# Half of an expert's first weight loaded earlier, and unread matmuls and a new order in the first units of a fused recurrence and mixture-of-experts kernel

## The chip, the cores and the metric

The kernel runs on one core of one Trainium2 chip. The metric is device time in microseconds (us) of one execution, taken as the median of several. PE is the matrix engine (PEld its weight loads), DVE the vector engine, ACT the scalar engine, POOL the GpSimd engine, SP the sync engine, which issues the loads of the two large inputs and the stores. POOL issues the loads of the expert weights, and these convert float32 to bfloat16 on the way.

## The reference

Two stages follow each other. The first is a gated recurrence over 5056 steps, for 4 sequences of 256 channels; the second is a soft mixture of experts with 8 experts of 4 slots each, over all 20224 tokens.

```python
sig = 1 / (1 + exp(-f_logit));  f = lb + (1 - lb) * sig
for t in range(S):  h = f[:, t] * h + (1 - f[:, t]) * x[:, t];  y[:, t] = h
logits = y @ phi                               # 20224 x 32
d = softmax(logits, over tokens);  slot_input = d.T @ y
slot_out[e] = relu(slot_input[e] @ w1[e]) @ w2[e]     # w1: 256x1024, w2: 1024x256
out = softmax(logits, over slots) @ slot_out
```

The inputs `x` and `f_logit` are 20.7 MB each, the weights 16.8 MB, the output 20.7 MB, all float32.

## The kernel before

The program has a stage that reads and a stage that writes. The sequences are cut into 10 groups of 512 steps; a group of one sequence is a unit, so that there are 40 units (`n_unit`). The loop `for n in range(n_unit)` writes the order of every engine by hand (`manual_schedule`), so that an instruction stands on its engine where the loop puts it.

What happens to a unit, in the order of its data:

- `load` (L207): SP loads `f_t` and `x_t`, six units ahead, into three buffers each. The first four units have loads of their own (`SINGLE` = 4), later ones go in pairs.
- `gate` (L226): ACT takes the sigmoid of `f_t` into `s_t`.
- `enter` (L236): POOL multiplies `s_t` by `x_t` into `u_t` (DVE does it for unit 0).
- `s_to_channels`, `u_to_channels` (L266, L275): PE turns both so that channels lie on partitions, into `sp` and `up` in PSUM. From unit 4 on a unit's `up` needs the `u_t` of both units of its pair (`half_to_channels`, L260).
- `decay` (L288): ACT makes the factors `a` from `sp`.
- `scan` (L323): DVE runs the recurrence, two scans of 512 steps for each unit (L332).
- `to_tokens`, `keep_tokens` (L339, L355): PE turns the result `h` back, and DVE or ACT copies it to `ht`.
- Then `logits`, `exps`, `weights_to_tokens` and `slots` add each group to `slot_ps`, one half of a PSUM bank.

The other half of that bank, `slot_bank[:, 1]`, takes matmuls that nobody reads: `idle(k)` (L177) puts k of them, `ident_f` by `wide_rep` with 256 columns in float32, into PE's order. `wide_rep` is a view of `rep`, which POOL builds in four copies (`rep_constants`, L84).

POOL issues the weight loads in its own order of work, after `enter(n + 3)` of the units that a table names. Entries 0 to 7 are `w1` of each expert, 8 to 15 are `w2`; the last `w2` goes in three pieces:

```python
W_AT = {9: 1, 17: 1, 25: 1, 31: 1, 32: 1, 33: 2, 34: 3, 36: 6}
```

After the last unit come the slot inputs (`sin_ps`, a part of the PSUM tile `tail`, in which PE also writes the row sums), the hidden layer (`hi`, from `w1`), its turned copies (`hid`, `wide`), the sums over `w2` (L684, and L696 into `so_ps`), `slot_out` (L708), and then the stage that writes: PE multiplies the stored weights of each token by `slot_out`, DVE and ACT scale the product by the row sums, SP stores it.

Of the kernel before, what the change touches and what calls it, by code (L numbers as in the profile page):

```python
# [18 lines left out]
def kernel(  # L19
# [10 lines left out]
    nc = tc.nc  # L30
# [5 lines left out]
    P = 128  # L36
# [47 lines left out]
    def rep_constants(b):  # L84
        blk = ident_f[ds(b * NS, NS), ds(b * NS, NS)]
        nc.gpsimd.tensor_copy(rep[ds(b * NS, NS)], blk.unsqueeze(1).broadcast_to([NS, B, NS]))
# [17 lines left out]
    def lb_constants():  # L104
        row = lb_row.rearrange("u (p o) -> u p o", o=DC)
        lb_ps = ptp.tile([P, R, P], F32, name="lb_ps", tag="tp")
        lb = lb_ps[:, 0, ds(0, DC)]
        for o in range(DC):
            nc.tensor.transpose(lb_ps[:, 0, ds(o, 1)], row[:, :, o], ident_f[ds(0, 1), ds(0, 1)])
        nc.vector.tensor_scalar(omlb, lb, -1.0, 1.0, ALU.mult, ALU.add)  # L110
        nc.vector.tensor_scalar(nomlb, lb, 1.0, -1.0, ALU.mult, ALU.add)
# [22 lines left out]

    def load_w(i):
        if i < E:
            nc.gpsimd.dma_start(out=w1_sb[i], in_=w1_r[i])
        else:
            if i == 2 * E - 2:
                t = ld.tile([P, 2, R, D], F32, name="w_t", tag="f_t")  # L140
                t = t.rearrange("p u r d -> p (u r d)").bitcast(BF16).rearrange(
                    "p (e f d) -> p e f d", e=2, f=FC)
                w2_sb.extend(t[:, i] for i in range(2))
            parts = (FC // 2, FC // 4, FC // 4) if i == 2 * E - 1 else (FC,)
            for j, k in enumerate(parts):
                f = sum(parts[:j])
                nc.gpsimd.dma_start(out=w2_sb[i - E][:, ds(f, k)], in_=w2_r[i - E][:, ds(f, k)])
# [14 lines left out]
    with tc.tile_pool(name="sp2", bufs=3) as sp2, \  # L162
# [11 lines left out]

        wide_rep = rep.rearrange("p b s -> p (b s)").unsqueeze(1).broadcast_to([P, 2, P])

        def idle(k, first=False):  # L177
            if first:
                for i in range(2):
                    nc.tensor.matmul(slot_bank[:, 1, ds(0, P)], ident, ident,  # L180
                                     start=True, stop=False, skip_group_check=True)
            for _ in range(k):
                nc.tensor.matmul(slot_bank[:, 1], ident_f, wide_rep,  # L183
                                 start=False, stop=False, skip_group_check=True)
        xs, fs, sts, uts, pss, psus, hs, hps, hts, lgs, ets = ({} for _ in range(11))

# [70 lines left out]
                nc.tensor.matmul(v[:, :, :, r], t(r)[k].bitcast(F32), sides,  # L257
                                 is_transpose=True, start=True, stop=True)

        def half_to_channels(n, ps, t):  # L260
            k = ds(n % 2 * (P // 2), P // 2)
            v = ps.rearrange("c p r -> c (p r)").rearrange("c (p r) -> c p r", r=2 * R)
            for r in range(2 * R):
                nc.tensor.transpose(v[:, :, r], t(r)[k].bitcast(F32), ident_f[k, k])  # L264

        def s_to_channels(n):  # L266
# [8 lines left out]
        def u_to_channels(n):  # L275
            ps = psu.tile([P, P, R], F32, name="up", tag="up")
            if long(n):
                half_to_channels(n, ps, lambda r: uts[n - n % 2 + r // R][:, r % R])
            elif n // B == odd:
                woven_to_channels(n, ps, lambda r: uts[n - n % 2 + r // R][:, r % R])  # L280
            else:
                to_channels(n, ps, uts[n])
            psus[n] = ps.rearrange("c p r -> c (p r)").bitcast(BF16).rearrange(
                "c (t o) -> c t o", o=DC)
# [149 lines left out]
        def unit(f, m):  # L434
            if 0 <= m < n_unit:
                f(m)
# [45 lines left out]
            load(n, 1)  # L482
        load(SINGLE)
        lb_constants()
        gate(0, 1)
        enter(0)
        s_to_channels(0)
        decay(0, 1, [0])
        u_to_channels(0)
        gate(1, 1)  # L490
        decay(0, 1, [1])
        phi_constants()
        enter(1)
        s_to_channels(1)
        u_to_channels(1)
        gate(2, 1)
        decay(1, 1)
        enter(2)
        for n in range(n_unit):
            if n < SINGLE - 2:  # L500
                if n:
                    unit(to_tokens, n - 1)
                    unit(u_to_channels, n + 1)
                s_to_channels(n + 2)
                if n + 3 < SINGLE:
                    gate(n + 3, 1)
                decay(n + 2, 1)
                if n + 3 == SINGLE:
                    gate(n + 3)
                if n % 2 == 0:  # L510
                    unit(load, n + AHEAD)
                unit(enter, n + 3)
                for b in range(2 * n, 2 * n + 2):
                    rep_constants(b)
            else:
                end = n >= n_unit - 6
                if n % 2 == 0:
                    unit(load, n + AHEAD)
                    if n == SINGLE - 2:
                        to_tokens(n - 1)  # L520
                        keep_tokens(n - 1)
                    if not end and n >= SETTLED:
                        unit(gate, n + 4)
                else:
                    unit(decay, n + 1)
                    if n in (late + 1, late + 3):
                        keep_tokens(n - 2)
                    if n < SETTLED:
                        gate(n + 3)
                    if n == n_unit - 5:  # L530
                        gate(n + 3)
                        exps(odd - 1)
                if not end and n != n_unit - 7:
                    group(exps, n - 2)

                unit(enter, n + 3)
                for _ in range(W_AT.get(n, 0)):
                    load_w(w_next[0])
                    w_next[0] += 1

                if n in (n_unit - 3, n_unit - 2):
                    unit(u_to_channels, n + 1)
                if n in (late, late + 2):
                    to_tokens(n - 2)
                elif n not in (SINGLE - 2, late - 1, late + 1):
                    unit(to_tokens, n - 1)
                if n == n_unit - 2:
                    keep_tokens(n - 1)
                if n % 2 == 0:
                    unit(s_to_channels, n + 2)  # L550
                    unit(s_to_channels, n + 3)
                if n not in (n_unit - 3, n_unit - 2):
                    unit(u_to_channels, n + 1)
                if n in (n_unit - 5, n_unit - 4):
                    idle(2)
                elif n == SINGLE - 2:
                    idle(1, True)
                elif 2 * B <= n < n_unit - 4 and n % (2 * B) in (1, 5, 6, 7):
                    idle(1)
                if n == n_unit - 2:  # L560
                    tail = psp.tile([P, 2, G], F32, name="tail", tag="sp")
                    sums = tail[:, 0]
                    rs_ps = sums[:, ds(0, n_grp * R * B)].rearrange(
                        "p (q b) -> p q b", b=B)
                    late_ps, odd_ps = (
                        tail[:, 1].bitcast(BF16)[:, ds(i * R * P, R * P)].rearrange(
                            "p (r s) -> p r s", r=R) for i in range(2))
                    logits(odd)
                    exps(odd)
                    slots(odd - 2)  # L570
                elif not end and by_pairs(n - 1):
                    if n % B == 0:
                        g = (n - 1) // (2 * B) * 2
                        for i in range(2):
                            logits(g + i, [2, 3] if n % (2 * B) == 0 else [0, 1])
                elif not end:
                    group(logits, n - 1)
            if n == n_unit - 1:
                odd_weights()
                logits(last, [0, 1, 2])  # L580

            unit(scan, n)
            if n in (late, late + 2):
                keep_tokens(n - 2)
                to_tokens(n - 1)
            elif n not in (SINGLE - 2, late - 1, late + 1, n_unit - 2):
                unit(keep_tokens, n - 1)
            if n == n_unit - 3:
                weights_to_tokens(odd - 1, nc.scalar.copy)
            elif not n >= n_unit - 6:  # L590
                group(weights_to_tokens, n - 3)
                batch(slots, n - 4, 0)
                batch(slots, n - 4, 1)
                if n > 2 * B and n % (2 * B) == 3:
                    idle(1)
# [17 lines left out]
        slot_sb = hpool.tile([P, G, DC], BF16, name="slot_sb", tag="h")  # L613
        slot_sb = slot_sb.rearrange("p t o -> p (t o)").bitcast(F32)[:, ds(0, D)]
        nc.vector.tensor_copy(slot_sb, slot_ps)
        sin_ps = tail[:, 0, ds(G // 2, DC * NS)].rearrange("p (o s) -> p o s", o=DC)
        slot_v = slot_sb.rearrange("p (c o) -> p o c", o=DC)
        for o in range(DC):
            nc.tensor.matmul(sin_ps[:, o], slot_v[:, o], rep[:, 0],
# [250 lines left out]
```

## Time and profile before

| what | value |
|---|---|
| median of 3 runs | 197.94 us (197.11, 197.94, 198.4) |
| the profiled execution, its own time | 197.01 us |
| its span, from the first to the last instruction | 195.2 us |
| busy share of the span: PE, DVE, ACT, POOL | 77%, 73%, 71%, 53% |
| read from HBM, written to it | 58.23 MB, 20.71 MB |
| mean granted clock of PE, as a share of full speed | 0.845 |

The span is 1.8 us shorter than the execution's own time. The shares are averages over two stages: up to about 142 us the kernel reads and computes, after it it writes. So the table says little by itself, and stages must be read one by one. In the views, a line "A <- B: 3.5, 2, 2.6" of waits says that A waited for B 3.5 us in total, 2 times, at most 2.6 us. In the table of stretches, each engine has its busy time and, as (x..), its number of instructions; behind them stand PE's granted clock, the mean busy share of the 16 DMA engines and GB/s moved. Those bytes are counted as they are written, so that a weight, read in float32 and written in bfloat16, counts half.

### The profile page before, as it was taken

The page shows a single profiled execution, that of the slowest core. Times are in us where ns is not written, and L with a number is a line of the kernel's source. Part 1 is how long each engine was busy: PE and PEld are TensorE (multiplying, and loading weights), DVE is VectorE, ACT ScalarE, POOL GpSimd, SP SyncE. Part 2 cuts the span into 40 slices and gives each one's busy share as a digit, 9 for nine tenths or more (in the row PEclk, how much of TensorE's full clock was granted, in tenths as well). Part 3 has the DMA queues.
Part 4 walks back from the last instruction along what each step waited for, and adds up shares of the span by engine and source line. Part 5 has one row for each costly group of instructions (what it writes and reads, how often), then busy time and mean ns, then how long its engine had stood idle before and what let it go on. Part 6 is the DMA issues. An engine that isn't in the chain of part 4 may idle for free.

```text
span 195.2 us, 3283 instructions
## 1 busy us (share of the span) xinstructions
PE 150.6 (77%) x1222; PEld 108.7 (56%) x1222; DVE 142.0 (73%) x175; ACT 138.8 (71%) x192; POOL 103.1 (53%) x78
## 2 busy tenths in 40 slices
PE   0684896898998979989798976999997999980000
PEld 0474775765786657857576755766872663420000
DVE  2666699799699999999999999824288867770000
ACT  3686778599988998989988698724068788991000
POOL 2584888756798949776888979592030000000000
PEclk9998799699699999999999999999985555555555
DMA  6999999999999999999999999999949999999995
GB/s 203 415 433 428 426 425 421 430 426 411 326 428 426 423 334 405 423 425 414 324 418 418 235 212 214 214 212 211 170 165 428 425 431 426 430 433 430 430 430 218
DMA packets 12145, 70.75 MB, mean 362 GB/s; under 512 B 1361, under 2 KB 1874, under 8 KB 7650
## 3 DMA queue, kind: packets, MB, share of 16 engines
q1 hardware_dynamic: 9504, 62.13, 76.3%
q0 software_dynamic: 2624, 8.42, 21.8%
q8 instruction: 9, 0.15, 0.3%
q14 instruction: 6, 0.05, 0.1%
q10 hardware_dynamic: 2, 0.00, 0.0%
HBM read 58.23 MB, written 20.71 MB: 404 GB/s over the span
## 4 chain that ended last, share of the span: by engine, by line
PE 36%; DVE 28%; DMA 17%; ACT 4%; issue 4%; SPq 1%; POOL 0%; ACTq 0%
DVE h L332 17%; DMA w_t<-in_moe_w_dram 7%; PE op L801 7%; PE sp L249 7%; PE op L727 6%; DMA w_sb<-in_moe_w_dram 6%; PE hp L345 5%; DVE ht L364 5%; PE up L264 4%; DMA f_t<-in_f_logit_dram 4%; DVE h L319 3%; DVE oc L717 2%; PE op L760 2%; ACT s_t L234 1%; PE lg L378 1%
## 5 line engine op out<-in xcount | busy, mean ns | idle before, releaser
L245 POOL TENSOR_TENSOR u_t<-s_t,x_t 128x1024 bf16<-128x1024 bf16 (+1 forms) x39 | 82.4, 2129 | 24.5 <-ACT s_t L234 14.2
L332 DVE TENSOR_TENSOR_SCAN h<-a,h,up 128x512 bf16<-128x512 f32 x64 | 78.1, 1267 | 9.0 <-PE up L264 4.3
L234 ACT ACTIVATE s_t<-f_t 128x2048 bf16<-128x2048 f32 (+2 forms) x22 | 38.1, 1736 | 2.9 <-DMA f_t<-in_f_logit_dram 2.9
L345 PE MATMUL hp<-ident_f,h 128*128 128x128 f32 (+1 forms) x160 | 29.3, 307 | 8.4 <-DVE ht L364 6.3
L297 ACT ACTIVATE a<-sp,lbs 128x1024 f32<-128x1024 bf16 x28 | 29.6, 1112 | 4.6 <-PE sp L249 4.5
L345 PEld LDWEIGHTS hp<-ident_f,h 128*128 128x128 f32 (+1 forms) x160 | 23.2, 206 | 17.0 <-DVE ht L364 11.5
L249 PE MATMUL sp<-ident_f,s_t 128*128 128x128 f32 x144 | 23.7, 315 | 7.0 <-ACT s_t L234 5.7
L249 PEld LDWEIGHTS sp<-ident_f,s_t 128*128 128x128 f32 x144 | 19.6, 164 | 8.7 <-ACT s_t L234 6.5
L264 PE MATMUL up<-ident_f,u_t 64*128 64x64 f32 x224 | 21.4, 236 | 2.4 <-POOL u_t L245 2.4
L264 PEld LDWEIGHTS up<-ident_f,u_t 64*128 64x128 f32 x224 | 17.0, 144 | 7.1 <-POOL u_t L245 2.8
L721 ACT ACTIVATE ob<-op,rrow 128x256 f32<-128x256 f32 x32 | 12.4, 478 | 9.1 <-PE op L727 8.7
L364 ACT COPY ht<-hp 128x512 f32<-128x512 f32 (+1 forms) x21 | 12.2, 583 | 7.9 <-PE hp L345 7.9
L304 ACT ACTIVATE a<-sp,lbs 128x512 f32<-128x512 bf16 (+2 forms) x16 | 13.2, 868 | 2.9 <-PE sp L249 2.7
L183 PE MATMUL slot_ps<-rep,ident_f 128*128 128x256 f32 x42 | 14.2, 426 | 0.0
L364 DVE COPY ht<-hp 128x512 f32<-128x512 f32 (+1 forms) x19 | 12.7, 668 | 1.0 <-PE hp L345 1.0
L801 PE MATMUL op<-slot_bd,etall 64*128 64x512 bf16 x32 | 13.1, 627 | 0.0
L812 ACT ACTIVATE oc<-op,rrow 128x256 f32<-128x256 f32 x32 | 12.2, 486 | 0.8 <-PE op L801 0.3
L727 PE MATMUL op<-slot_out,etall 32*128 32x256 bf16 x64 | 12.6, 375 | 0.1
L806 DVE TENSOR_TENSOR oc<-op,rrow 128x1024 f32<-128x1024 f32 x8 | 9.7, 1223 | 3.4 <-PE op L801 3.4
L717 DVE TENSOR_TENSOR ob<-op,rrow 128x1024 f32<-128x1024 f32 (+2 forms) x12 | 9.8, 862 | 2.2 <-DMA out_dram<-ob 1.1
L727 PEld LDWEIGHTS <-etall 32*128 32x128 bf16 x64 | 8.9, 153 | 3.8 <-issue 1.3
L378 PE MATMUL lg<-h,phi 128*32 128x512 bf16 (+1 forms) x80 | 9.9, 389 | 0.2 <-ACT et L402 0.2
(109 smaller groups left out, 168.9 us busy)
## 6 DMA issues: line engine op xcount, KB each, us to landing
f_t<-in_f_logit_dram SPq DMA_DIRECT2D x14, 1024.0 KB, 11.2
x_t<-in_x_dram SPq DMA_DIRECT2D x14, 1024.0 KB, 9.5
out_dram<-oc SPq DMA_DIRECT2D x4, 2048.0 KB, 13.1
w_sb<-in_moe_w_dram POOLq DMA_DIRECT2D x14, 512.0 KB, 9.5
out_dram<-ob SPq DMA_DIRECT2D x3, 2048.0 KB, 9.6
f_t<-in_f_logit_dram SPq DMA_DIRECT2D x8, 512.0 KB, 7.0
x_t<-in_x_dram SPq DMA_DIRECT2D x8, 512.0 KB, 6.1
out_dram<-oc SPq DMA_DIRECT2D x4, 896.0 KB, 6.0
```

The source lines that it names most:

```text
L183: nc.tensor.matmul(slot_bank[:, 1], ident_f, wide_rep, start=False, stop=False, skip_group_check=True)
L234: nc.scalar.activation(s_t, f_t, ACT.Sigmoid, scale=-1.0)
L245: nc.gpsimd.tensor_tensor(uts[n][:, :r], s_t[:, :r], x_t[:, :r], ALU.mult)
L249: nc.tensor.transpose(ps[:, :, r], t[:, r].bitcast(F32), ident_f)
L264: nc.tensor.transpose(v[:, :, r], t(r)[k].bitcast(F32), ident_f[k, k])
L297: nc.scalar.activation(a, sp[:, :, :, :, o], ACT.Identity, scale=nomlb[:, ds(o, 1)], bias=1.0)
L332: nc.vector.tensor_tensor_scan(h[:, :T, o], decays[n // 2, o][:, n % 2, :T], up[:, :T, o], hs[number(g - 1, b)][:, ds(used(g - 1) - 1, 1), ...
L345: nc.tensor.transpose(hp[:n_p, r], hw[:, :n_p, r], ident_f)
L364: copy(hts[g][:n_p, b].rearrange("p r d -> p (r d)").bitcast(F32), hps.pop(n)[:n_p].rearrange("p r c -> p (r c)"))
L717: nc.vector.tensor_tensor(ob, op, scale.broadcast_to(list(ob.shape)), ALU.mult)
L727: nc.tensor.matmul(op[:, j], ew[:, :, r + j], slot_out[ds(b * NS, NS)], start=True, stop=True, skip_group_check=True)
L801: nc.tensor.matmul(op[:, i_r].rearrange("p u d -> p (u d)"), ew[:, :, r + i_r], slot_bd[ds(j * 2 * NS, 2 * NS)].rearrange("s u d -> s (u d)"),
```

## The change

Four things are edited together.

1. **Half a weight.** `w1` of the last expert lies in SBUF as two halves (`o` = 0 and 1). Half 0 is now loaded by a DMA of its own, behind the other work of unit 13 on POOL; at its old place, unit 34, only half 1 is loaded. The loads stay 58.23 MB in all, with one DMA more.
2. **Unread matmuls.** `idle` gets a parameter for what streams; `plain` is `ident_f` itself, which is there before `rep`. Three go ahead of unit 0 (with the two that open the bank, which stood at unit 2), two behind `u_to_channels(0)`, one ahead of `u_to_channels(1)`, four ahead of `s_to_channels(4)`. With `wide_rep`, one follows the transposes of units 3, 5 and 7 in the loop (as one at unit 2 already did), and two stand between the halves of `u_to_channels(12)`. That is 15 more matmuls.
3. **Split gate, reordered constants.** The gate of units 4 and 5 becomes two, of one unit each. At `n == 1`, POOL's copies into `rep` come ahead of `enter(4)`, not behind it.
4. **Another place for `sin_ps`.** It moves from `tail` to `slot_bank[:, 1]`.

```diff
@@ load_w
         if i < E:
-            nc.gpsimd.dma_start(out=w1_sb[i], in_=w1_r[i])
+            o = ds(int(i == E - 1), DC - int(i == E - 1))
+            nc.gpsimd.dma_start(out=w1_sb[i][:, o], in_=w1_r[i][:, o])
@@ idle
+        plain = ident_f.unsqueeze(1).broadcast_to([P, 2, P])
-        def idle(k, first=False):
+        def idle(k, first=False, moving=wide_rep):
...
-                nc.tensor.matmul(slot_bank[:, 1], ident_f, wide_rep,
+                nc.tensor.matmul(slot_bank[:, 1], ident_f, moving,
@@ half_to_channels (rests is true for unit 12)
             for r in range(2 * R):
+                if r == R and rests:
+                    idle(2)
@@ ahead of the loop
         lb_constants()
+        idle(3, True, plain)
         gate(0, 1)
...
         u_to_channels(0)
+        idle(2, moving=plain)
         gate(1, 1)
...
         s_to_channels(1)
+        idle(1, moving=plain)
         u_to_channels(1)
@@ in the loop, n < SINGLE - 2
                 if n + 3 == SINGLE:
-                    gate(n + 3)
+                    gate(n + 3, 1)
+                    gate(n + 4, 1)
...
-                unit(enter, n + 3)
+                if n == 0:
+                    unit(enter, n + 3)
                 for b in range(2 * n, 2 * n + 2):
                     rep_constants(b)
+                if n:
+                    unit(enter, n + 3)
@@ in the loop, n >= SINGLE - 2
                     w_next[0] += 1
+                if n == 13:
+                    nc.gpsimd.dma_start(out=w1_sb[E - 1][:, 0], in_=w1_r[E - 1][:, 0])
...
+                if n == SINGLE - 2:
+                    idle(4, moving=plain)
                 if n % 2 == 0:
                     unit(s_to_channels, n + 2)
...
-                elif n == SINGLE - 2:
-                    idle(1, True)
+                elif n in (SINGLE - 2, SINGLE - 1, SINGLE + 1, SINGLE + 3):
+                    idle(1)
@@ after the loop
-        sin_ps = tail[:, 0, ds(G // 2, DC * NS)].rearrange("p (o s) -> p o s", o=DC)
+        sin_ps = slot_bank[:, 1, ds(0, DC * NS)].rearrange("p (o s) -> p o s", o=DC)
```

More of the change, by code (lines that the diff above doesn't have):

```diff
@@ L258, in woven_to_channels, with half_to_channels @@
                                  is_transpose=True, start=True, stop=True)
-        def half_to_channels(n, ps, t):
+        def half_to_channels(n, ps, t, rests=False):
             k = ds(n % 2 * (P // 2), P // 2)
@@ L277, in u_to_channels @@
             if long(n):
-                half_to_channels(n, ps, lambda r: uts[n - n % 2 + r // R][:, r % R])
+                half_to_channels(n, ps, lambda r: uts[n - n % 2 + r // R][:, r % R],
+                                 n == 3 * B)
             elif n // B == odd:
```

## The prediction

> **What bounds the kernel now.** I read the page's slices first, then a table of stretches, then the chain of waits near the end, then what each stage waits for.
>
> From the page, the granted clock and the DMA engines in 40 slices of 4.88 us, and the bytes:
>
> ```profile
> PEclk9998799699699999999999999999985555555555
> DMA  6999999999999999999999999999949999999995
> HBM read 58.23 MB, written 20.71 MB: 404 GB/s over the span
> ```
>
> The DMA row is at 9 from the second slice on, but for one slice and the last: the transfers pause only at the change from reading to writing. The clock dips three times in the first eleven slices. The table of stretches sets both beside the engines:
>
> ```profile
> 3.00:15.00 12.00, 8.02 (x33) 6.11 (x34) 6.88 (x9) 7.68 (x10) 7.38 (x5) 1.00 1.03 422
> 15.00:18.50 3.50, 0.84 (x7) 0.64 (x5) 2.63 (x3) 3.06 (x3) 1.06 (x3) 1.00 1.01 426
> 18.50:22.00 3.50, 3.48 (x16) 3.20 (x16) 0.87 (x2) 1.48 (x2) 3.22 (x4) 0.51 1.02 433
> 35.50:39.00 3.50, 3.50 (x20) 3.06 (x19) 2.11 (x2) 1.51 (x3) 3.33 (x2) 0.51 1.00 424
> 49.30:52.70 3.40, 3.40 (x21) 2.65 (x20) 1.89 (x2) 3.40 (x4) 2.87 (x2) 0.51 1.04 304
> 52.70:100.00 47.30, 43.10 (x416) 32.79 (x416) 46.24 (x44) 43.75 (x42) 38.42 (x20) 1.00 1.02 401
> 126.00:141.00 15.00, 14.52 (x221) 10.91 (x214) 5.07 (x14) 3.98 (x10) 5.90 (x7) 1.00 1.05 205
> 141.00:144.30 3.30, 2.90 (x28) 2.45 (x27) 1.90 (x5) 1.26 (x4) 1.66 (x2) 1.00 0.04 8
> ```
>
> The DMA share is 1.00 or more in every stretch up to 141 us, in the three of half clock too. Where GB/s falls (304, 205) weights are under way, which count half; the share does not fall. So the reading is one unbroken transfer of 58.23 MB, and it ends at 141 us. DVE is busy 46.24 of the 47.30 us after 52.7: from there the scans have no slack either. The end of reading, in the chain of waits (start, length, what) and in PE's timeline:
>
> ```profile
> 115.00 11.64 DMA w_sb<-in_moe_w_dram
> 126.64 0.28 issue
> 126.92 14.59 DMA w_t<-in_moe_w_dram
> 141.52 0.04 issue
> 141.56 0.39 PE so_ps L696 x2
> ```
>
> ```profile
> 139.50 1.79 PE L696 MATMUL so_ps<-w_t,wide 128*128 128x256 bf16 x14
> 141.56 0.38 PE L696 MATMUL so_ps<-w_t,wide 128*128 128x256 bf16 x2 [0.27 <-DMA w_t<-in_moe_w_dram]
> ```
>
> The last piece of weights lands at 141.52 us and releases the last two matmuls; the output follows from them. But PE had its other 14 done at 141.29 and stood only 0.27 us. Two chains end together: the transfers (141.52) and the computing (0.27 us before). A gain needs both to shorten; a loss needs one to lengthen.
>
> **Part 1, half a weight moved.** The bytes stay. Moving half of 1.05 MB forward puts everything behind it later by its own duration and everything behind the old place where it was. Sizes, from the page's list of issues (last column: us from issue to landing):
>
> ```profile
> f_t<-in_f_logit_dram SPq DMA_DIRECT2D x14, 1024.0 KB, 11.2
> w_t<-in_moe_w_dram POOLq DMA_DIRECT2D x1, 512.0 KB, 15.9
> w_t<-in_moe_w_dram POOLq DMA_DIRECT2D x1, 256.0 KB, 16.7
> ```
>
> The whole `w_t` is issued at 123.03 and lands at 138.9; five full loads land between 126.64 and 138.9, 2.45 us each. The half-size piece, issued at 123.55, lands at 140.25, 1.3 us later, where half of 2.45 is 1.22. So a half costs 0.1 us more than half a whole, and two halves cost **+0.2 us** at the end of reading. Bounds: 0 (no loss per piece) and +0.4 (twice that).
>
> The two halves raise the number of DMAs by one. [...]
>
> On POOL the new issue takes 0.58 us (as at 65.62), in a stretch in which POOL multiplies from 49.83 to 62.55 without a break; `enter(17)` and those behind it start that much later. The `f_t` and `x_t` behind the half land 1.22 us later. An `x_t` of 1 MB issued at 54.11 lands at about 61.2, and `enter(20)`, which reads it, starts at 63.52: 2.4 us of slack hide both (1.8 together). Gone that slack, up to 1.8 us reach the scans. The half's semaphore makes POOL wait for the first weight load, which is long over at unit 34, so nothing queues there.
>
> **Part 2, 15 unread matmuls.** Their price is the row of those that are there:
>
> ```profile
> L183 PE MATMUL slot_ps<-rep,ident_f 128*128 128x256 f32 x42 | 14.2, 426 | 0.0
> ```
>
> Ten with `plain` lie at or before 18.5 us: 4.3 us, beside 4.0 and 2.7 us in which PE is idle in the first two stretches above; I take them as hidden (uncovered: up to 4.3). The five with `wide_rep` come at about 27, 32, 37 and 47 us, where PE's waits before the next transposes are 0.4 to 1.1 us: 2.1 us, of which I take half as hidden, bounds 0 and 2.1 (4.0 at half clock, where eight `sp` transposes took 1.97 us instead of 1.04).
>
> What they can remove is what DVE loses to slow transposes before 53 us:
>
> ```profile
> DVE h L332 <- PE up L249: 3.5, 2, 2.6
> DVE h L332 <- PE up L264: 3.1, 2, 1.6
> ```
>
> The first waits belong to the stretch at 18.5 us, the others to those at 35.5 and 49.3. In each of the latter two, the transposes (`hp` 1.0 for 0.75, `sp` 1.9 for 1.04, `up` 1.1 for 0.71) take 1.5 us longer than at full clock, so that the gain is at most 3.1 us there, and in the first 1.7 (next part). The least is 0, if the half-clock stretches stay.
>
> **Part 3, gate and constants.** A gate of two units took 1.91 us (16.56 to 18.47), one of one unit 1.06. Split, unit 4 has its `s_t` at 17.62, 0.85 earlier, and unit 5 at 18.68, 0.2 later. POOL's two copies (0.61 us) move into the 2.48 us in which it waited for that gate, so that `enter(5)` ends about 1.7 us earlier. With part 2 this lets the scan of unit 3 start at 19.7 instead of 21.44.
>
> **Part 4, `sin_ps`.** DVE waited 1.49 us for row sums in the same tile before `sin` (131.21). That wait goes, but the hidden layer's matmuls stand behind those row sums (to 131.1) and started at 131.52: 0.4 us at most, on the computing side.
>
> **The sum.** Computing: between 1.7 + 3.1 + 0.4 = 5.2 us earlier and 2.1 later, most likely 1 to 3 us earlier. Reading: 0.2 us later. The end is the later of the two. A computing chain that is earlier only lengthens PE's 0.27 us of waiting; the 141.52 becomes 141.7, and what follows (0.39 + 0.49 us, then 20.71 MB of output, DMA share 1.01) is untouched. Span 195.2 + 0.2 = 195.4; the execution's own time 197.01 + 0.2 = 197.2. That execution is the fastest of four (the runs: 197.11, 197.94, 198.4). With 0.27 us between the chains, one in which computing falls 1 us later ends 1 us later; with the change such a delay has slack. So I put the median nearer to 197.2 than to 197.94 + 0.2, at **197.4 us**.
>
> **The rivals.**
>
> *Computing is the only bound, and faster.* For it: DVE's 98% after 52.7 us, and 5.2 us to be had. Against it: the unbroken DMA share. If it held, the gain would be limited by when inputs land, 2.4 us at unit 20: 197.0 - 2.4 = 194.6 us. [...]
>
> *The unread matmuls hold PE up, slower.* Place: the five with `wide_rep`, in PE's order ahead of the transposes that the scans wait for. After 52.7 us DVE can regain nothing, so the delay reaches `so_ps` whole; it decides once it exceeds the 0.27 us of slack. Price 2.1 - 0.3 = 1.8 us, 198.8 us; with all five at half clock 3.7, 200.7. Against it: the same edit should shorten the three waits above by more.
>
> *The half starves the scans.* Without the 2.4 us of slack (used up by a faster start), 1.8 - 0.3 = 1.5 us: 198.5 us. Against it: a faster start is then what pays for it.
>
> *The clock dips stay.* Then parts 2 and 3 do nothing they seem made for; the time is that of the forecast, since reading sets it.
>
> **How the numbers follow.** Forecast (dips gone or not) 0.74, computing bound 0.08, unread matmuls 0.10, starving 0.08. The forecast's own range is 196.5 to 198.4, half a per cent around it, from the spread of the runs; for 8 in 10 I reach to 199.2, over the starving case and the lower half of the held-up one, and leave out 194.6 and 200.7. A change of 1%, 2 us, is about what a measurement here tells from none. Faster by that needs the first rival, 0.07; slower needs the upper half of the held-up PE or something unseen, 0.07; the rest, 0.86, is within.
>
> **What would show it.** Right: the DMA share at 1.0 up to 141 us; the last `w_t` landing within 0.4 us of 141.52; PE waiting for it longer than 0.27 us; fewer slices of low clock before 53 us, with DVE's waits for `up` shorter; an output stage of unchanged length. Wrong: the last weight landing over 1 us earlier or later, a DMA share under 0.95 in a stretch before 140, or `so_ps` ending behind the last landing for want of `wide` or `hi`.

## The result, and the profile after

| | before, same chip | after |
|---|---|---|
| median (runs) | 197.53 us (6: 196.81 to 198.5) | 199.78 us (6: 198.98 to 201.1) |
| the profiled execution, its own time | 197.01 us | 199.16 us |
| its span | 195.2 us | 197.4 us |
| granted clock of PE | 0.845 | 0.870 |

The changed kernel is slower: the ratio is 1.0118, 95% interval 1.0075 to 1.0162. The forecast was 197.4 us within 196.5 to 199.2, so the result lies outside it, on the slow side. All that follows compares the two profiled executions, which differ by 2.15 us.

The page of the changed kernel: instructions of each engine, the granted clock and the DMA share in 40 slices (now 4.94 us each), and one queue that the prediction never looked at (packets, MB, share of 16 engines).

```profile
PE 153.0 (78%) x1252; PEld 109.7 (56%) x1252; DVE 142.1 (72%) x175; ACT 139.1 (70%) x193; POOL 103.6 (52%) x79
PEclk9999879999999999999999999999996555555555
DMA  5999999999999999999999999999559999999992
q8 instruction: 10, 0.16, 0.3%
```

The clock dips once in the first eleven slices, not three times, and falls for good at the change to writing, as before. PE and PEld have 30 instructions more each. Queue q8 has ten packets, where the page of the kernel before says:

```profile
PE 150.6 (77%) x1222; PEld 108.7 (56%) x1222; DVE 142.0 (73%) x175; ACT 138.8 (71%) x192; POOL 103.1 (53%) x78
q8 instruction: 9, 0.15, 0.3%
```

The stretches of the changed kernel (us; busy time and instructions of PE, PEld, DVE, ACT, POOL; clock; DMA share; GB/s):

```profile
18.50:22.00 3.50, 2.11 (x17) 1.73 (x15) 2.66 (x3) 3.15 (x3) 3.50 (x2) 1.00 1.04 440
35.50:39.00 3.50, 3.50 (x31) 2.36 (x30) 3.50 (x4) 2.61 (x4) 2.89 (x2) 1.00 0.99 419
49.30:52.70 3.40, 3.40 (x44) 2.44 (x42) 3.07 (x4) 3.40 (x4) 3.40 (x2) 1.00 1.04 328
126.00:141.00 15.00, 12.21 (x195) 9.43 (x188) 4.82 (x13) 2.48 (x7) 5.90 (x7) 1.00 1.04 205
```

The three stretches that ran at 0.51 now run at 1.00 (the dip that is left lies between 22 and 35.5 us, clock 0.87). Before the end PE has less left to do: 12.21 us of work in the last 15 us of reading, where it had 14.52. The DMA share is still 1.0. The chain of waits of the changed kernel at the end of reading, and the same place in PE's timeline:

```profile
127.13 15.56 DMA w_t<-in_moe_w_dram
142.69 0.04 issue
142.73 0.39 PE so_ps L713 x2
```

```profile
140.31 2.15 PE L713 MATMUL so_ps<-w_t,wide 128*128 128x256 bf16 x14 [2.55 <-DMA w_t<-in_moe_w_dram]
142.73 0.38 PE L713 MATMUL so_ps<-w_t,wide 128*128 128x256 bf16 x2 [0.27 <-DMA w_t<-in_moe_w_dram]
```

PE now stands 2.55 us for a weight. Transfers set the end even more plainly than before, but the last weight lands at 142.69 instead of 141.52: **1.17 us later**. The first store is issued 2.06 us behind that landing in both kernels. From there to the landing of the last store it was 50.44 us (143.58 to 194.02) and is 51.42 (144.75 to 196.17): **0.98 us longer**, in a stage in which no instruction of the kernel was changed. The two add up to 2.15 us, the whole loss.

### The profile page after: what moved, and what is told of

It reads as the page before. It is cut to its first block, busy times and chain, and to the rows that moved or that the text cites. A ratio compares the mean times of both kernels' runs of the same rounds, so it can differ in the third digit from the quotient of the medians.

```text
span 197.4 us, 3345 instructions
## 1 busy us (share of the span) xinstructions
PE 153.0 (78%) x1252; PEld 109.7 (56%) x1252; DVE 142.1 (72%) x175; ACT 139.1 (70%) x193; POOL 103.6 (52%) x79
## 3 DMA queue, kind: packets, MB, share of 16 engines
HBM read 58.23 MB, written 20.71 MB: 400 GB/s over the span
## 4 chain that ended last, share of the span: by engine, by line
PE 28%; DMA 23%; DVE 18%; ACT 10%; POOL 5%; issue 4%; ACTq 0%; SPq 0%; POOLq 0%
DVE h L338 11%; DMA x_t<-in_x_dram 9%; DMA w_t<-in_moe_w_dram 8%; DMA w_sb<-in_moe_w_dram 7%; PE op L818 7%; PE op L744 6%; POOL u_t L248 5%; PE up L269 4%; PE sp L252 4%; PE hp L351 4%; DVE ht L370 3%; DVE h L325 3%; ACT s_t L237 3%; ACT oc L784 2%; PE slot_ps L186 2%
## 5 line engine op out<-in xcount | busy, mean ns | idle before, releaser
L351 PE MATMUL hp<-ident_f,h 128*128 128x128 f32 (+1 forms) x160 | 28.7, 302 | 6.3 <-DVE ht L370 4.1
L252 PE MATMUL sp<-ident_f,s_t 128*128 128x128 f32 x144 | 20.7, 286 | 3.1 <-ACT a L310 1.5
L252 PEld LDWEIGHTS sp<-ident_f,s_t 128*128 128x128 f32 x144 | 17.3, 148 | 5.4 <-ACT s_t L237 3.0
L186 PE MATMUL slot_ps<-rep,ident_f 128*128 128x256 f32 x52 | 17.3, 423 | 0.0
L338 DVE TENSOR_TENSOR_SCAN h<-a,up 128x512 bf16<-128x512 f32 x8 | 9.4, 1210 | 1.4 <-PE up L269 0.8
```

The costliest lines, as they stand in the source:

```text
L186: nc.tensor.matmul(slot_bank[:, 1], ident_f, moving, start=False, stop=False, skip_group_check=True)
L252: nc.tensor.transpose(ps[:, :, r], t[:, r].bitcast(F32), ident_f)
L338: nc.vector.tensor_tensor_scan(h[:, :T, o], decays[n // 2, o][:, n % 2, :T], up[:, :T, o], hs[number(g - 1, b)][:, ds(used(g - 1) - 1, 1), ...
L351: nc.tensor.transpose(hp[:n_p, r], hw[:, :n_p, r], ident_f)
```

## The experiments

**The theories.** The two losses have one thing in common, queue q8. Each of its packets brings 16 KB (0.15 MB in 9, 0.16 MB in 10). The kernel before has 9 for 2444 instructions of PE and PEld, the changed one 10 for 2504: one in some 250 to 270. Each takes 0.88 to 0.98 us of one of the 16 DMA engines' time in these two traces. The times of these packets, from the trace:

| | in reading | between | in writing |
|---|---|---|---|
| before | 8, the last at 135.27 us | 1 at 141.24 | none |
| after | 9, the last at 138.11 us | none | 1 at 168.34 |

The fetch at 141.24 counts as between the stages: the last packet of the weights had ended by 141.20 us, though the landing is marked at 141.52.

*Fetch theory*: the 15 unread matmuls are 60 more instructions of PE (each is two weight loads and two matmuls: PE goes from 1222 to 1252, and so does PEld); so all fetches move forward, one from the gap into the reading, and one is new in the writing. Both stages are full (in the kernel before, a DMA share of 1.00 or more in every stretch from 3 to 141 us, 0.97 or more from 146 to 188 us), so a fetch should hold up whatever else its engine carries, and a transfer that is spread over all engines with it; signs of that follow. Places where it can be seen: from the weights' landing at 136.68 to the next of the same size it took 3.58 us instead of 2.45, with the fetch of 138.11 between. Two stores of 2 MB landed 4.96 us apart before (164.59, 169.55) and 6.20 us after (165.77, 171.97), with the fetch of 168.34 between.

The trace also holds sixteen landing signals of each of these transfers, as many as there are DMA engines; the landing times in this document (142.69, 171.97 and the others) are those of the last of the sixteen. Of the weight that landed at 140.26, the last signal came 1.51 us behind the median of the sixteen, and the one before it 0.38. Of the store of 171.97 it was 1.86, and 0.60. In the kernel before, the last signal of the store of 169.55 came 0.62 us behind. In the writing the lag stays to the end: in the last store it is 1.78 us, where the latest of the kernel before is 0.81 us behind. So behind each of these two fetches one signal of sixteen is late, which I read as one engine; in the writing 1.0 us of its lag shows, because another was 0.8 us late in any case (0.79 in the last store).

*Rivals*: the half weight breaks the stream of loads more dearly than 0.1 us a piece; the unread matmuls hold PE up by their time; the new order of the first units, or the new place of `sin_ps`, shifts the loads.

**Part 1 alone.** The kernel before with the first two hunks on the half (`load_w`, and the DMA behind unit 13).

```diff
-            nc.gpsimd.dma_start(out=w1_sb[i], in_=w1_r[i])
+            o = ds(int(i == E - 1), DC - int(i == E - 1))
+            nc.gpsimd.dma_start(out=w1_sb[i][:, o], in_=w1_r[i][:, o])
...
+                if n == 13:
+                    nc.gpsimd.dma_start(out=w1_sb[E - 1][:, 0], in_=w1_r[E - 1][:, 0])
```

> Part 1 alone: half of the last expert's first weight behind unit 13, nothing else changed. PE's instructions are as before. Fetch theory (PE's own instructions are fetched 16 KB at a time through the same DMA engines; the changed kernel has 60 PE instructions more, which puts one more fetch into the reading stage and one into the writing stage, 1 us each): no change, 197.5 us within 0.4. Half theory (the smaller pieces and their place in the queue make the reading end 1.2 us later): 198.5 to 199.

Measured: 197.19 us against 196.97; ratio 1.0021, interval 1.0000 to 1.0042. The last weight lands at 141.60, the writing takes 50.43 us, the fetches are 8, 1 and 0 in the three columns. The interval for the cost of the half reaches from nothing to 0.8 us, and in the profiled execution the last weight lands only 0.08 us later than before. So it starves nothing, and the later weight of the changed kernel is not its doing.

**The change without part 1.** The changed kernel with those hunks taken back.

```diff
-            o = ds(int(i == E - 1), DC - int(i == E - 1))
-            nc.gpsimd.dma_start(out=w1_sb[i][:, o], in_=w1_r[i][:, o])
+            nc.gpsimd.dma_start(out=w1_sb[i], in_=w1_r[i])
...
-                if n == 13:
-                    nc.gpsimd.dma_start(out=w1_sb[E - 1][:, 0], in_=w1_r[E - 1][:, 0])
```

> The changed kernel without part 1: unread matmuls, split gate, constants and the slot-input tile stay, the weight is loaded whole again. Fetch theory: the loss stays whole, +2.0 to +2.3 us, 199.5 to 199.9, with the same two fetches at about 138 and 168 us. Half theory: the reading ends as before, so at most the +1.0 of the writing stage stays, 198.5 or less.

Measured: 199.28 us against 196.97; ratio 1.0113, interval 1.0096 to 1.0129. The loss stays (a little less than the 199.5 to 199.9 us expected). The last weight lands at 142.42, the writing takes 51.29 us, the fetches are 9, 0 and 1 (138.15 and 168.88). In this execution the first store came 2.97 us behind the last weight and not 2.06, for another reason. PE's last products (first line) and the stretch in which they ran (second line):

```profile
140.27 3.48 PE L710 MATMUL so_ps<-w_t,wide 128*128 128x256 bf16 x16 [2.33 <-DMA w_t<-in_moe_w_dram]
140.20:143.80 3.60, 3.53 (x20) 2.60 (x20) 0.01 (x1) 0.00 (x0) 0.00 (x0) 0.54 0.17 28
```

The clock fell to 0.54 there, and the sixteen products took 3.48 us, against 2.15 + 0.38 in the changed kernel at a clock of 1.00; so here PE finished behind the last weight. It had waited 2.33 us before them, and in the changed kernel 2.55: the length of a wait does not tell by itself whether the clock falls.

**Parts 3 and 4 alone.** The kernel before with the split gate, the constants ahead of `enter`, and `sin_ps` in `slot_bank[:, 1]`.

```diff
-                    gate(n + 3)
+                    gate(n + 3, 1)
+                    gate(n + 4, 1)
...
-                unit(enter, n + 3)
+                if n == 0:
+                    unit(enter, n + 3)
                 for b in range(2 * n, 2 * n + 2):
                     rep_constants(b)
+                if n:
+                    unit(enter, n + 3)
...
-        sin_ps = tail[:, 0, ds(G // 2, DC * NS)].rearrange("p (o s) -> p o s", o=DC)
+        sin_ps = slot_bank[:, 1, ds(0, DC * NS)].rearrange("p (o s) -> p o s", o=DC)
```

> Parts 3 and 4 alone: split gate, reordered constants, the slot-input tile in the other bank. No PE instruction more, no DMA more. Fetch theory: eight fetches in the reading stage and none in the writing stage, so no loss; computing is 1 to 2 us earlier and reading still ends at 141 to 141.5, so the time is that of before, 196.8 to 197.1, PE waiting 1 us or more for the last weights. Order theory (the new order of POOL and ACT or the bank of the slot inputs is part of the loss): 198 or more.

Measured: 197.02 us against 197.05; ratio 0.9999, interval 0.9972 to 1.0026. Its chain of waits ends as that of the kernel before:

```profile
127.00 14.56 DMA w_t<-in_moe_w_dram
141.56 0.04 issue
141.60 0.39 PE so_ps L700 x2
```

The last weight lands at 141.56 us, and nothing is gained. Of the four parts, the unread matmuls are left.

**60 instructions and nothing else.** The kernel before with 30 unread matmuls of one column, in bfloat16 (a weight load and a matmul each), ahead of unit 0. They touch no load, and no transpose behind unit 0.

```diff
         lb_constants()
+        for _ in range(30):
+            nc.tensor.matmul(slot_bank[:, 1, ds(0, 1)], ident, ident[:, ds(0, 1)],
+                             start=True, stop=True, skip_group_check=True)
         gate(0, 1)
```

> The kernel before with 30 matmuls of one column (60 PE instructions) ahead of unit 0, where PE waits for the first gate; they feed nothing. No byte, no order of any other engine and no place of an unread matmul changes. Fetch theory: the whole loss appears, 199.5 to 199.9 us, with a fetch near 140 us and one near 170. Half theory and order theory: no change, 197.5.

Measured: 198.74 us (198.67 to 199.11) against 196.97; ratio 1.0090, interval 1.0077 to 1.0104. The loss is here again, 1.8 us of it, without the change; it is less than the 199.5 to 199.9 us expected, since the last weight is 0.76 us late here and not 1.17. The last weight lands at 142.28, the writing takes 51.40 us, the fetches are 9 (the last at 138.63), 0 and 1 (167.91). Two stretches of 0.4 us of this kernel, at the end of its reading:

```profile
141.20:141.60 0.40, 0.40 (x4) 0.28 (x3) 0.00 (x0) 0.00 (x0) 0.00 (x0) 1.00 0.08 13
141.60:142.00 0.40, 0.37 (x3) 0.19 (x2) 0.00 (x0) 0.00 (x0) 0.00 (x0) 1.00 0.06 10
```

A DMA share of 0.06 is one engine of sixteen: all others have finished, and the last weight waits for that one. The changed kernel shows the same:

```profile
141.60:142.00 0.40, 0.40 (x4) 0.28 (x3) 0.00 (x0) 0.00 (x0) 0.00 (x0) 1.00 0.06 10
142.00:142.40 0.40, 0.40 (x3) 0.19 (x2) 0.00 (x0) 0.00 (x0) 0.00 (x0) 1.00 0.08 13
```

The kernel before does not; its weight has landed at 141.52:

```profile
141.60:142.00 0.40, 0.40 (x7) 0.38 (x7) 0.02 (x1) 0.00 (x0) 0.00 (x0) 1.00 0.00 0
```

**60 instructions in the writing stage.** The same 30 matmuls in that stage (they run from 162.0 to 162.8 us), so that no fetch in the reading is moved.

```diff
             whole(0, b)
+        op = pout.tile([P, R, D], F32, name="op", tag="op")
+        for _ in range(30):
+            nc.tensor.matmul(op[:, 0, ds(0, 1)], ident, ident[:, ds(0, 1)],
+                             start=True, stop=True, skip_group_check=True)
```

> The kernel before with 30 matmuls of one column (60 PE instructions) in the writing stage, behind the first four blocks of output. Nothing changes ahead of them. Fetch theory: eight fetches in reading as before, one in the writing stage at 165 to 178 us, the store under way then lands about 1.2 us late and all later ones with it: +0.9 to +1.1 us, 197.9 to 198.1. If a fetch costs nothing: 197.0. If the 30 matmuls themselves held the output up, the DMA share of the writing stage would fall below 0.95 somewhere; I expect 0.99 or more.

Measured: 197.96 us against 197.05, +0.91 us by the medians; ratio 1.0031, interval 1.0003 to 1.0058 (a few scattered executions of both kernels widen it). Queue q8 of this kernel in the three parts of the span (3 to 141, 141 to 144.3, 144.3 to 196 us):

```profile
q8 instruction: 8, 0.13, 0.3%
```
```profile
q8 instruction: 1, 0.02, 1.8%
```
```profile
q8 instruction: 1, 0.02, 0.1%
```

The first two are those of the kernel before, which has none in the third. The last weight lands at 141.54, as before; the writing takes 51.40 us, +0.96, with the fetch at 167.78, and there the two stores landed 6.02 us apart (164.78, 170.80). From 146 to 188 us, in stretches of 6 us, the DMA share stays at 0.98 or more (0.97 or more in the kernel before), so that the 30 matmuls do not themselves hold the output up.

**16 instructions.** As the 60 ahead of unit 0, but with eight matmuls.

```diff
+        for _ in range(8):
+            nc.tensor.matmul(slot_bank[:, 1, ds(0, 1)], ident, ident[:, ds(0, 1)],
...
```

> The kernel before with 8 matmuls of one column (16 PE instructions) ahead of unit 0. Too few for a tenth fetch, so the writing stage keeps its length. The ninth fetch stood at 141.24, 0.1 us behind the end of reading; 16 PE instructions earlier, at two per 0.13 us of the last sums, it comes at 140 to 140.7, within reading. Fetch theory: +0.3 to +1.0 us, 197.3 to 198.0, less than the +1.8 of 60 instructions. Without it: 197.0.

Measured: 197.67 us (197.06 to 201.04) against 197.05; ratio 1.0020, interval 0.9993 to 1.0047. Inconclusive: the interval holds no change. The profiled execution, 199.19 us, is no help with the time: its transfers fell to 358 GB/s between 56 and 66 us (427 in the kernel before), for a reason that its trace does not show. Its ninth fetch, at 142.34, came 1.37 us ahead of the last landing, and none of the sixteen signals stands out there (the last is 0.80 us behind the median, the next 0.75). So a late fetch does not always show.

**Two ways to have the instructions back.** The changed kernel with all unread matmuls in bfloat16, which leaves x1216 on PE (one fewer for each of the 36):

```diff
-        wide_rep = rep.rearrange("p b s -> p (b s)").unsqueeze(1).broadcast_to([P, 2, P])
-        plain = ident_f.unsqueeze(1).broadcast_to([P, 2, P])
+        wide_rep = plain = ident.unsqueeze(1).broadcast_to([P, 2, P])
...
-                nc.tensor.matmul(slot_bank[:, 1], ident_f, moving,
+                nc.tensor.matmul(slot_bank[:, 1], ident, moving,
```

> The changed kernel with every unread matmul (old and new, 36) in bfloat16 instead of float32, the identity by itself: one weight load and one matmul each instead of two of both, so 72 PE instructions fewer than the changed kernel and 12 fewer than before. Fetch theory: the ninth fetch falls into the gap between reading and writing again and the tenth goes; 197.0 to 197.7, the loss gone. Half theory, or one that blames the new order or the unread matmuls' places: 199 to 200 as the changed kernel. The unread matmuls are shorter, so low-clock stretches may come back; they should not matter, since reading sets the end.

And the changed kernel without 16 of the old unread matmuls, x1220 (the expectation says 17, and 8 instructions fewer than the kernel before; PE and PEld have 2 fewer each):

```diff
-                elif 2 * B <= n < n_unit - 4 and n % (2 * B) in (1, 5, 6, 7):
-                    idle(1)
...
-                if n > 2 * B and n % (2 * B) == 3:
-                    idle(1)
```

> The changed kernel without 17 of the unread matmuls that were there already (those of the loop from unit 8 on), so that PE has 8 instructions fewer than in the kernel before and all four parts of the change are kept. Fetch theory (60 more PE instructions bring one more fetch of instructions into the reading and one into the writing stage): the late fetch falls behind the end of reading again and none is in the writing stage; last weight 141.5 to 141.8 us, writing stage 50.4 us, 197.0 to 197.4 us. It holds if PE's clock stays at full speed from 53 to 141 us; if the clock drops there, computing ends last, and the end of reading and the length of the writing stage are the figures to read. Rival (something else in the order of the first units, or the half, makes the loss): 198.8 to 199.8 us, last weight about 142.7 and writing stage 51.4 us as in the changed kernel.

Measured: 198.91 us (197.41 to 200.74), ratio 1.0115, interval 1.0082 to 1.0149, and 199.70 us (197.31 to 201.07), ratio 1.0136, interval 1.0091 to 1.0181, both against some 196.97. The numbers forecast for the medians, 197.0 to 197.7, were missed. The profiled executions, the fastest of each, say why:

| | fetches | last weight | writing | own time |
|---|---|---|---|---|
| bfloat16 | 8, 1, 0 | 141.93 us | 50.44 us | 197.41 us |
| 16 fewer | 8, 1, 0 | 141.58 us | 50.44 us | 197.31 us |

Both stages have their old lengths back, as the fetch theory has it. But the end is now set by something else; the chain of waits of the kernel with 16 fewer:

```profile
139.61 2.65 PE so_ps L709 x24
142.29 0.49 DVE slot_out L721
```

The 24 products run on end, with no wait for a weight, and finish 0.7 us behind the last landing: the computing ends last. These kernels lack a part of the unread work; in the long stretch of the scans PE is busy 38.70 of 47.30 us (16 fewer) and 40.05 (bfloat16), where it was 43.10 in the kernel before and 43.44 in the changed one, and its clock is 0.93 in both, here with 16 fewer,

```profile
52.70:100.00 47.30, 38.70 (x369) 30.30 (x369) 44.35 (x42) 42.55 (x41) 37.93 (x21) 0.93 1.02 395
```

where it is 1.00 in the kernels before and after. Over the executions of the bfloat16 kernel the mean clock is 0.817 to 0.839 (after: 0.846 to 0.870). So these two runs bear the theory out by the lengths of the stages in one execution each, and not by the time: each undoes two things at once, and the longer executions have no profile. No version beat the kernel before.

## Why the prediction was wrong, point by point

- **Reading sets the end; two chains.** Right, and the reason why the gains were worth nothing. DVE's wait for `so_ps` ahead of `slot_out` grew from 2.4 to 5.7 us; 1.17 of these 3.3 us are the later weight, and the other 2.1 are the computing that was done earlier, within the forecast's 1 to 3. A rival that let the time follow the computing (194.6 us) is refuted.
- **Part 1, +0.2 us.** Not contradicted, but too small to be resolved: alone it measured +0.22 us by the medians, with an interval that begins at nothing, and 0.08 us at the last weight. That the half starves the scans is refuted by the same run.
- **Part 2, the step that failed.** The 15 unread matmuls were priced by PE's time alone, 426 ns each (that is the row's mean for one instruction; a matmul is two, which took 0.70 us together at 48.04 in the kernel before), and set against PE's idle time. By that reckoning they were nearly free, and as far as PE's time goes they were. Not counted was that they are 60 instructions, which queue q8 brings in packets of 16 KB (10 now, 9 before), through the very DMA engines that the same text had found full in every stretch. The sentence "what follows is untouched" and the 141.7 us for the end of reading fell with it: +1.17 and +0.98 us, where +0.2 and 0 stood. Shown is that 60 instructions of another kind, in the kernel before, bring both delays (1.8 us), and that 60 placed in the writing bring the second alone (0.9 us). The row that would have raised the question was on the page: nine packets on the queue of instructions, for 2 x 1222 instructions of PE and PEld.
- **Their benefit.** Right in kind: the three dips went, and one new one came. DVE's waits for `up` ahead of 53 us went from 6.6 us, in the two rows shown before, to 5.7, and the longest from 2.6 to 1.8: shorter, as forecast, but by 0.9 us, at the low end of the 0 to 4.8 us (1.7 + 3.1) that the forecast allowed.
- **Part 3.** The scan of unit 3 starts at 19.34 us (forecast 19.7; before 21.44). **Part 4**: DVE's wait ahead of `sin` fell from 1.5 to 0.9 us. Both real, both on the side that does not set the end.
- **The rival "unread matmuls hold PE up"** named the right part, and its 198.8 to 200.7 us holds the result; its mechanism is another. At the end PE waits 2.55 us for a weight, so that PE's own time is not what sets it; that the result falls in this rival's range is chance.
- **The range** was made of the spread of the runs and of delays on engines; no bound had been put on what the instructions themselves cost to fetch. Of the 2.25 us between the medians, 1.8 are matched by the 60 instructions alone; the rest, some 0.5, is within the spread of the runs (198.98 to 201.1), and how much of it is the half is not resolved.

## What to carry to other kernels

Here, with the DMA engines full, 60 instructions cost 1.8 us although they stand where PE waits in any case (1.96 us for the first gate, in the kernel before). So where the DMA engines are full, read the queue of instructions on the page of the profile, divide the engine's instruction count by its packets, and see in which stage the next packet would fall. Two ideas follow from this that no run here has shown: unread matmuls that are there for the clock (three stretches went from 0.51 to 1.00) might better be few long instructions, and a saving could lie in pushing a fetch out of a full stage into a gap. And two stages that grow by the same 1 us, one of them unchanged in code, point to something that lies below both.

## What the runs showed of the hardware

A fetch of 16 KB held up the full stream of stores by about 1 us, far more than its share of the bytes (16 KB of 20.71 MB written would be 0.04 us): the writing took 50.43 to 50.44 us in six profiled executions without one and 51.29 to 51.42 in four with one. The 60 instructions in the writing stage are 30 matmuls that ran within 0.8 us; the stage was 0.96 us longer, with a DMA share of 0.98 or more in each stretch of 6 us from 146 to 188 us. So where the DMA engines were full, that fetch was not hidden behind other work.

The eight earlier fetches in the reading do not seem to cost 1 us each, since all kernels have them and read at 1.0 of the DMA engines' time. The traces show two ways in which one can be free. In the kernel before, the last packet of the weights had ended by 141.20 us when the fetch of 141.24 began. And in the reading a lag can be made up: in the run with 16 instructions, one signal of the weight that landed at 136.89 came 1.60 us behind the median, after the fetch of 134.82; at the next weight the last was 0.93 us behind, beside another at 0.87. Which engine takes a fetch is not in the records, so they do not tell beforehand which fetch will show.
